# Transfers of the turned weights cut into parts and released by TensorE, in threshold attention followed by a bilinear FFN

## The chip, the cores and the metric

The kernel runs on one core of one Trainium2 chip. The metric is the device time of one execution in microseconds (us); less is better.

## The reference

```python
# 8 batches, 8 heads, 576 rows, head size 64; 4608 tokens, d_model 512, d_ff 1536; all float32
scores = scale * np.matmul(q, k.transpose(0, 1, 3, 2))
thresh = np.max(scores, axis=-1, keepdims=True) - tau
scores = np.where(scores >= thresh, scores, -1000000000.0)
scores = scores - np.max(scores, axis=-1, keepdims=True)
attn = np.exp(scores)
attn = attn / (np.sum(attn, axis=-1, keepdims=True) + 1e-09)
attn_out = np.matmul(attn, v)
x = np.ascontiguousarray(attn_out.transpose(0, 2, 1, 3)).reshape(B * S, H * D)
out = (x @ w_a) * (x @ w_b) @ w_out
```

## The kernel before, in words

Two heads of one batch make a **pair**; there are 32 pairs, four to a batch. The 576 query rows of a pair are handled as four **units** of 128 rows (u = 0 to 3) and one of 64 rows (u = 4, the tail). A list written out by hand orders the 160 units: for the first batch u = 0 and 1 of all four pairs, then u = 2 and 3 of each pair, then the four tails; for every later batch u = 0, 1 of each of its pairs, then u = 2, 3 and the tail of each. So a batch takes 20 units, and batches begin at units 20, 40, 60 and so on.

The main loop runs over **slots** g, one unit each. `keep_order` pins every engine to the order in which the program issues its instructions, so that what is written here as "later in the slot" is later in the queue of that engine. In slot g:

- `scores` (L325) multiplies q by k for unit g into two PSUM tiles `sc`, and VectorE takes the row maxima (L332).
- `turn_back` issues the load of `wT`, the turned weights of a part whose pieces have been written to the DRAM scratch `swap` (L460). `exchange_blocks` follows.
- `turn_blocks` transposes the 32x32 blocks of unit g-1 on VectorE (L429, for a tail L442) and, for u = 1 and u = 3, issues four DMAs of 288 KB `swap<-tw` (L437); for a tail it issues four of 72 KB (L449). `tw` is the tile in which the weights of two neighbouring units lie side by side. It has two buffers, so that the weights two tiles on may be written only when these DMAs have read theirs. Also the four tails of the first batch share one `tw` tile; later tails have a tile `wt` of one buffer.
- `advance(PORTIONS[0] * pace)` runs a share (0.3) of the FFN work due in this slot. The FFN is a generator whose products (`pab` L574, `po` L617 and L661) fill TensorE between the attention's own.
- `weigh` lets ScalarE compute exp (L359, L360) and VectorE mask and sum (L363), which frees the two `sc` tiles. Then `prep` transposes q and k of a coming pair, `advance` runs another share (0.35), and `weighted` multiplies the turned weights of unit g-4 by v (`pv`, L475), where that unit completes a part.
- The weights are normalised (L382). Then come the loads of q or k for a coming pair (L143, four DMAs of 72 KB), of v (L158, 288 KB) and the stores of finished rows (L685), and `advance` twice (0.15 and 0.2).

q is loaded four slots ahead of its pair's first unit and k three slots ahead; for a batch that begins at slot G these loads lie in the slots G-4 to G+3, q in the even ones and k in the odd ones. The first eight units of the first batch are turned on TensorE instead (`turn_pe`) and use no `swap`.

All of these DMAs but two small ones at the start are issued by SyncE, whose queue is called SPq in the profile. A `wT` load must wait until the `swap` writes that it reads have landed, and SPq stands still during such a wait. PSUM has four tiles (`banks`), handed out in turn to `sc`, `pab`, `pv` and `po`.

Of the kernel before, what the change touches and what calls it, by code (L numbers as in the profile page):

```python
# [51 lines left out]
def kernel(  # L52
# [38 lines left out]
    nc = tc.nc  # L91
    B, H, S, D = q.shape
    P = 128
    Q = 32
# [317 lines left out]
    def part(i, u):  # L412

        if i < HP:
            return {1: (i, 0), 3: (i, 1), NT: (i, 2)}.get(u)
        return {1: (i, 0), NT: (i, 1)}.get(u)

    def width(i, h):
        return (HALF, HALF, TAIL)[h] if i < HP else (HALF, HALF + TAIL)[h]

    def turn_blocks(i, u):

        ws, _ = weights.pop((i, u))
        if u < NT:
            if u % 2 == 0:
                tbufs[i] = state["tw"]
            tb = tbufs[i]
            for w in ws:
                nc.vector.transpose(w, w)  # L429
            if u % 2 == 0:  # L430
                return
            h = u // 2
            n = width(i, h)
            swap = scratch.tile([2 * NB, Q, n], FP32, tag=f"swap{n}", name="swap")
            swaps[i, h] = swap
            for g in range(G):
                nc.sync.dma_start(  # L437
                    swap[:, :, g * 2 * Q:(g + 1) * 2 * Q].rearrange("c p w -> p c w"),
                    tb[g * Q:(g + 1) * Q])
        else:  # L440
            tb = ws[0]
            nc.vector.transpose(tb, tb)  # L442
            if i < HP:
                swaps[i, 2] = scratch.tile([2 * NB, Q, TAIL], FP32, tag="swapt", name="swap")
            swap = swaps[part(i, u)]
            for g in range(G):
                c = slice((1 - g // 2) * NB, (2 - g // 2) * NB)
                w0 = swap.shape[2] - TAIL + (g % 2) * Q
                nc.sync.dma_start(swap[c, :, w0:w0 + Q].rearrange("c p w -> p c w"),  # L449
                                  tb[g * Q:(g + 1) * Q])  # L450
        if part(i, u):
            ready.append(part(i, u))

    def turn_back():

        while ready:
            i, h = ready.pop(0)
            n = width(i, h)
            wT = work.tile([P, NSLOT, n], FP32, tag="wT", bufs=WT_BUFS, name="wT")
            nc.sync.dma_start(wT, swaps.pop((i, h)).rearrange("(s r) p w -> (r p) s w", r=G))  # L460
            turned[i, h] = wT

    def join(out, lo, hi):
        nc.scalar.copy(out, lo)
# [44 lines left out]
    def weighted(i, h):  # L509

        b, hp = pairs[i]
        n = width(i, h)
        pv = product(turned.pop((i, h)), loaded[i]["v"], n)
        if h < 2:
            if hp == 0:
                x_of[b, h] = x_tile("xT")
            lo, hi = (pv[:, r, 0:HALF].rearrange("p (i t e) -> p i t e", t=2, e=Q) for r in range(2))
            join(x_of[b, h][:, hp, :].rearrange("p (t i e) -> p i t e", t=2, e=Q), lo, hi)
            if hp == HP - 1:
                complete.append((x_of.pop((b, h)), ("half", b, h)))  # L520
        if n % HALF:
            t = b % GT
            if hp == 0 and t == 0:
                xtail_of[b // GT] = x_tile("xt")
            join(xtail_of[b // GT][:, hp, t * TAIL:(t + 1) * TAIL], pv[:, 0, n - TAIL:n], pv[:, 1, n - TAIL:n])
            del loaded[i], prepared[i]
            if hp == HP - 1 and t == GT - 1:
                complete.append((xtail_of.pop(b // GT), ("tail", b - t, 0)))
# [166 lines left out]
    def advance(cols):  # L695
        running["owed"] += cols
        while running["owed"] > 0:
            if running["ffn"] is None:
                if not blocks:
                    running["owed"] = 0.0  # L700
                    return
                running["ffn"] = ffn(*blocks.pop(0))
                running["left"] = cost()
            step, rest, whole = next(running["ffn"], (None, 0, 0))
            if step == 0:
                running["owed"] = 0.0
                return
            if step is None:
                running["ffn"] = None
                state["through"] += 1  # L710
            else:
                running["owed"] -= step
                running["left"] -= step
                running["done"] = running["done"] + step if rest else 0
                running["rest"] = rest
                running["room"] = min(ROOM, whole // 2)

    def make_room():

        while running["rest"] and not (running["done"] >= running["room"] <= running["rest"]):  # L720
            owed = running["owed"]
            running["owed"] = 0.0
            advance(1)
            running["owed"] += owed - 1
# [35 lines left out]
    for g in range(len(units) + PV_LAG):  # L760
        written = len(pending)
        state["converted"] = state["added"]
        here = g < len(units)
        converting = bool(early.get(g)) or bool(early.get(g - 1))
        if here:
            i, u = units[g]
            scores(i, u)
        turn_back()
        exchange_blocks()
        pace = (PACE if g > BY_PE else PACE_EARLY) * BLOCK_COLS  # L770
        if g > BY_PE:
            pace = min(pace, backlog() / (min([a for a in arrivals if a > g] + [len(units) + PV_LAG + 1]) - g))
        pace += (NSLOT + 1) // 2 * S / (NT + 1) + CATCH_UP * max(backlog() - BLOCK_COLS, 0)
        if 2 <= g < BY_PE + 2:
            weighted_unit(*units[g - 2])
            running["owed"] -= (NSLOT + 1) // 2 * P
        if g < 3:
            prep_copy(*prep_pe(g + 1, "q"))
        convert_rest(g, 0)
        if g == 3:  # L780
            for c in range(0, NSUM - 2 * CW + 1, 2 * CW):
                extra.append(sums_u32[:, c:c + 2 * CW].rearrange("p (f w) -> p f w", w=2))
        load_weights(RAWS)
        if g > BY_PE and g <= len(units):
            turn_blocks(*units[g - 1])
        if g > BY_PE:
            advance(PORTIONS[0] * pace)
        if here:
            weigh(i, u)
        if here and g < BY_PE:  # L790
            reciprocal(i, u, nc.vector)
        if 0 < g <= BY_PE:
            turn_pe(*units[g - 1])
        if g < 3:
            prep_copy(*prep_pe(g + 1, "k"))
        for p in range(HP, NPR):
            for name, d in (("q", 2), ("k", 1)):
                if g == first[p] - d:
                    prep(p, name)
        if g > BY_PE:  # L800
            advance(PORTIONS[1] * pace)
            n = g - PV_LAG
            if BY_PE <= n < len(units) and part(*units[n]):
                make_room()
                weighted(*part(*units[n]))
                running["owed"] -= (NSLOT + 1) // 2 * width(*part(*units[n]))
        for n in early.get(g, [])[:1]:
            convert_first(n)
            convert_clamp(n)
        if here and g < BY_PE:  # L810
            diagonals(i, u)
        elif here:
            reciprocal(i, u, nc.scalar if converting else nc.vector)
            normalise(i, u)
        convert_rest(g, 1)
        if g <= BY_PE:
            advance(pace)
        convert_rest(g, 2)
        for n in early.get(g, [])[1:]:
            convert_first(n)  # L820
            convert_clamp(n)
        load_weights(RAWS)
        for p in range(HP, NPR):
            for name, d in (("q", 4), ("k", 3)):
                if g == first[p] - d:
                    load(p, name)
        for p in range(1, NPR):
            if g == first[p] - 1:
                load_v(p)
        store(written)  # L830
        if g > BY_PE:
            advance(PORTIONS[2] * pace)
            advance(PORTIONS[3] * pace)

        if not converting and not state["sums"]:
            state["slots"] = state.get("slots", 0) + 1
            for n in {1: (0,), 2: (1,), 3: (2,)}.get(state["slots"], ()):
                for z in range(2):
                    weight_sums(n, z)
            if state["slots"] >= 3 and state["through"]:  # L840
                for z in range(2):
                    weight_sums(3, z)
                state["sums"] = True
# [38 lines left out]
```

## Time and profile before

| | |
|---|---|
| median of 3 runs | 1473.05 us (1471.87 to 1476.86) |
| span of the profiled execution | 1471.9 us |
| TensorE busy (PE) | 1420.3 us, 97% of the span |
| VectorE (DVE), ScalarE (ACT), GpSimd (POOL) busy | 942.8, 678.4, 334.6 us |
| DMA queue of SyncE | 216.52 MB in 621968 packets, 67.6% of 16 engines' span |
| `swap<-tw` | 240 DMAs of 288 KB, median 5.2 us from issue to landing |
| `swap<-tw` and `swap<-wt` of tails | 16 and 112 DMAs of 72 KB, 4.3 and 2.5 us |
| `wT<-swap` | 28 of 1440 KB, 7.7 us; 32 of 1152 KB, 6.2 us; 4 of 288 KB, 4.0 us |

The profile lists no device time of its own for the profiled execution beside this span; the span agrees with the lowest of the three runs and is 1.2 us below their median. A DMA that is issued on SyncE shows on SPq with the time that the issue took, which includes the time for which the queues were too full to take it; when its data landed is told apart.

### The profile page before, as it was taken

To read this page: it belongs to the slowest core of one execution; us is meant where nothing else is said; L and a number is where in the kernel's file an instruction comes from. 1 tells how busy PE (TensorE), PEld (TensorE's weight loads), DVE (VectorE), ACT (ScalarE), POOL (GpSimd) and SP (SyncE) were. 2 spreads that over 40 slices of the span, in tenths; PEclk is the share of its full clock that TensorE was granted. 3 is DMA by queue.
4 is the path that set the end of the run, shared out by engine and by line. 5 is a ranking of instruction groups with operands and counts; after the bars stand their busy time and mean duration, and the time that the engine had idled before them with its cause. 6 is when DMAs were issued, how large, how long until landed. Compare 5 with 4: busy or idle time off the path is not lost.

```text
span 1471.9 us, 57132 instructions
## 1 busy us (share of the span) xinstructions
PE 1420.3 (97%) x25344; PEld 1210.9 (82%) x25344; DVE 942.8 (64%) x2097; ACT 678.4 (46%) x1243; POOL 334.6 (23%) x504
## 2 busy tenths in 40 slices
PE   5878999999999999999999999999999999999998
PEld 4777677887879898897888998889888888888886
DVE  5998677677766875776656765577656766613212
ACT  5886455555544554544434544354544544411010
POOL 2773503122030403031212212120404040410000
PEclk9999999999999999999999999999999999999999
DMA  9977898789858876895647876588757977530000
GB/s 189 223 187 187 176 179 193 169 173 185 198 143 166 184 191 142 168 192 141 147 97 147 180 172 149 118 189 185 161 126 143 197 169 162 132 90 16 2 17 16
DMA packets 624582, 220.75 MB, mean 150 GB/s; under 512 B 542928, under 2 KB 612048, under 8 KB 624336
## 3 DMA queue, kind: packets, MB, share of 16 engines
q1 hardware_dynamic: 621968, 216.52, 67.6%
q8 instruction: 199, 3.26, 0.9%
q10 hardware_dynamic: 2368, 0.59, 0.2%
q14 instruction: 47, 0.39, 0.1%
HBM read 127.40 MB, written 89.65 MB: 147 GB/s over the span
## 4 chain that ended last, share of the span: by engine, by line
PE 86%; DVE 6%; DMA 3%; issue 1%; ACT 1%; SPq 1%; DVEq 0%; ACTq 0%
PE pab L574 47%; PE po L617 19%; PE sc L325 10%; PE pv L475 9%; PE po L661 1%; DVE mx L332 1%; DVE tw L363 1%; DVE tw L429 1%; DMA swap<-tw 1%; SPq L437 1%; DMA sums_u<-in_moe_w_a_dram 1%; DVE low L238 1%; DMA kT<-in_k_dram 0%; DMA wT<-swap 0%; PE tp L402 0%
## 5 line engine op out<-in xcount | busy, mean ns | idle before, releaser
L332 DVE TENSOR_REDUCE mx<-sc 128x1 f32<-128x576 f32 x288 | 205.2, 749 | 116.5 <-PE sc L325 105.7
L574 PE MATMUL pab<-xS,wa_sb 64*64 64x256 f32 (+1 forms) x3584 | 274.4, 373 | 1.9 <-issue 1.8
L574 PE MATMUL pab<-xS,wb_sb 64*64 64x256 f32 (+1 forms) x3584 | 266.6, 369 | 0.0
L325 PE MATMUL sc<-kT,qT 64*64 64x288 f32 x2304 | 243.4, 410 | 20.7 <-DVE kT L312 9.1
L574 PE MATMUL pab<-xT,wa_sb 64*64 64x256 f32 (+1 forms) x3200 | 238.2, 370 | 7.2 <-DVE tw L363 3.2
L586 POOL TENSOR_TENSOR h<-h 128x256 f32<-128x256 f32 x168 | 117.3, 732 | 548.0 <-PE po L617 544.9
L617 PE MATMUL po<-wo_sb,h 64*64 64x256 f32 x3264 | 240.7, 376 | 0.0
L574 PE MATMUL pab<-xT,wb_sb 64*64 64x256 f32 (+1 forms) x3200 | 237.0, 369 | 3.6 <-DVE h L582 2.2
L382 ACT ACTIVATE tw<-tw,rcp 128x576 f32<-128x576 f32 x244 | 176.1, 768 | 133.8 <-DVE rcp L376 133.6
L360 ACT ACTIVATE tw<-sc,bias,scalars 128x576 f32<-128x576 f32 x260 | 216.3, 832 | 17.4 <-DMA swap<-tw 6.5
L574 PEld LDWEIGHTS pab<-xS,wa_sb 64*64 64x64 f32 x3584 | 196.6, 134 | 29.7 <-issue 3.0
L363 DVE SCALAR_TENSOR_TENSOR tw<-sc,thr,tw 128x576 f32<-128x576 f32 x260 | 203.8, 802 | 22.5 <-ACT tw L360 21.8
L574 PEld LDWEIGHTS pab<-xS,wb_sb 64*64 64x64 f32 x3584 | 194.1, 133 | 23.0 <-issue 0.2
L574 PEld LDWEIGHTS pab<-xT,wa_sb 64*64 64x64 f32 x3200 | 171.9, 133 | 31.1 <-DVE kept L465 4.3
L617 PEld LDWEIGHTS po<-wo_sb,h 64*64 64x64 f32 x3264 | 177.7, 132 | 23.6
L574 PEld LDWEIGHTS pab<-xT,wb_sb 64*64 64x64 f32 x3200 | 172.3, 133 | 25.2 <-DVE h L582 2.4
L475 PE MATMUL pv<-wT,vm 64*64 64x320 f32 (+3 forms) x2592 | 186.8, 377 | 1.7 <-DVE h L582 1.7
L325 PEld LDWEIGHTS sc<-kT,qT 64*64 64x64 f32 x2304 | 145.2, 134 | 52.4 <-issue 17.2
L617 PE MATMUL po<-sums_u,h 64*64 64x256 f32 x2448 | 180.9, 376 | 0.0
L429 DVE STREAM_TRANSPOSE tw<-tw 128x576 f32<-128x576 f32 x240 | 171.6, 753 | 0.0
L582 DVE TENSOR_TENSOR h<-h,pab 128x512 f32<-128x512 f32 (+1 forms) x112 | 73.4, 655 | 145.3 <-PE pab L574 140.3
L475 PEld LDWEIGHTS pv<-wT,vm 64*64 64x64 f32 x2592 | 143.6, 133 | 20.9 <-DVE h L582 2.6
(83 smaller groups left out, 1240.8 us busy)
## 6 DMA issues: line engine op xcount, KB each, us to landing
swap<-tw SPq DMA_DIRECT2D x240, 288.0 KB, 5.2
wT<-swap SPq DMA_DIRECT2D x28, 1440.0 KB, 7.7
wT<-swap SPq DMA_DIRECT2D x32, 1152.0 KB, 6.2
vm<-in_v_dram SPq DMA_DIRECT2D x32, 288.0 KB, 4.8
qT<-in_q_dram SPq DMA_DIRECT2D x112, 72.0 KB, 3.6
kT<-in_k_dram SPq DMA_DIRECT2D x112, 72.0 KB, 4.9
swap<-wt SPq DMA_DIRECT2D x112, 72.0 KB, 2.5
out_dram<-kept SPq DMA_DIRECT2D x30, 256.0 KB, 4.7
```

The costliest lines, as they stand in the source:

```text
L238: nc.vector.scalar_tensor_tensor(out=low, in0=hi, scalar=0x80000000, in1=low, op0=ALU.bitwise_and, op1=ALU.bitwise_or)
L325: nc.tensor.matmul(sc[j if u < NT else 0][to, c], qT[r, q0:q0 + D], kT[r, c * SH:(c + 1) * SH], start=True, stop=True)
L332: nc.vector.tensor_reduce(mx[:, c], sc[j], axis=AX.XY, op=ALU.max)
L360: nc.scalar.activation(wb[j], sb[j], AF.Exp, bias=bias[:, j:j + 1], scale=e_scale)
L363: nc.vector.scalar_tensor_tensor(out=wv, in0=sb[j], scalar=thr[:, j:j + 1], in1=wv, op0=ALU.is_ge, op1=ALU.mult, accum_out=sums[:, j:j + 1])
L382: nc.scalar.activation(w, w, AF.Copy, scale=rcp[:, j:j + 1])
L429: nc.vector.transpose(w, w)
L475: nc.tensor.matmul(pv[j * D:(j + 1) * D, r], vm[rows, k0], wT[rows, k0], start=(s == (NT if j == r else 0)), stop=(s == NT - 1))
L574: nc.tensor.matmul(pab[c * D:(c + 1) * D, r], w[rows, f // n, k, fs + c * D:fs + (c + 1) * D], moving, start=(k == 0), stop=(k == H - 1))
L582: nc.vector.tensor_tensor(ht, ht, pab, op=ALU.mult)
L586: (nc.vector if state["over"] else nc.gpsimd).tensor_tensor(*a, **kw)
L617: nc.tensor.matmul(po[c * D:(c + 1) * D, r, y], ht[rows, t0:t0 + D], other[rows, f], start=(f == 0), stop=(f == NF // 2 - 1))
```

## The change

The DMAs of the turned weights are no longer issued where they are made. They are put in a list `bulk`: each of the four 288 KB writes of a `swap` as an item of its own, the four 72 KB writes of a tail together as one item, and each `wT` load cut into three items of three slots (480, 384 or 96 KB each). A new function `pump` takes the oldest item, looks up the TensorE instruction that the program issued last, and issues the item's DMAs with a semaphore wait of the first of them on that instruction. `pump` is called at four places of a slot from slot 9 on: after `turn_blocks`; after the first `advance`; after `weighted`, ahead of the loads of q, k and v and of the stores; and between the last two `advance`. Ahead of `weighted`, what is left of the part that it needs is issued at once.

```diff
             for g in range(G):
-                nc.sync.dma_start(
-                    swap[:, :, g * 2 * Q:(g + 1) * 2 * Q].rearrange("c p w -> p c w"),
-                    tb[g * Q:(g + 1) * Q])
+                bulk.append((None, [(swap[:, :, g * 2 * Q:(g + 1) * 2 * Q].rearrange("c p w -> p c w"),
+                                     tb[g * Q:(g + 1) * Q])]))
...
+            bulk.append((None, []))
             for g in range(G):
...
-                nc.sync.dma_start(swap[c, :, w0:w0 + Q].rearrange("c p w -> p c w"),
-                                  tb[g * Q:(g + 1) * Q])
+                bulk[-1][1].append((swap[c, :, w0:w0 + Q].rearrange("c p w -> p c w"), tb[g * Q:(g + 1) * Q]))
...
-            nc.sync.dma_start(wT, swaps.pop((i, h)).rearrange("(s r) p w -> (r p) s w", r=G))
+            rows = swaps.pop((i, h)).rearrange("(s r) p w -> (r p) s w", r=G)
+            for s in range(0, NSLOT, 3):
+                bulk.append(((i, h), [(wT[:, s:s + 3], rows[:, s:s + 3])]))
             turned[i, h] = wT
+
+    bulk = []
+
+    def pump(count=1):
+
+        for _ in range(min(count, len(bulk))):
+            behind = next(x.name for x in reversed(nc.cur_bb.bb.instructions) if x.engine == mybir.EngineType.PE)
+            for n, (out_, in_) in enumerate(bulk.pop(0)[1]):
+                done = nc.sync.dma_start(out_, in_)
+                if n == 0:
+                    tc.add_manual_dep(
+                        done.ins, behind,
+                        mybir.DependencyInfo(mybir.DependencyClass.Sync, mybir.DependencyReason.DATA),
+                        reason="pace")
...
             turn_blocks(*units[g - 1])
         if g > BY_PE:
+            pump()
             advance(PORTIONS[0] * pace)
+            pump()
         if here:
             weigh(i, u)
...
                 make_room()
+                while part(*units[n]) in [whose for whose, _ in bulk]:
+                    pump()
                 weighted(*part(*units[n]))
                 running["owed"] -= (NSLOT + 1) // 2 * width(*part(*units[n]))
+            pump()
...
             advance(PORTIONS[2] * pace)
+            pump()
             advance(PORTIONS[3] * pace)
```

## The prediction

> **What bounds the kernel now.** I read the page's busy shares and its chain first, then the windows of a few stretches, then the timeline of SyncE's queue and of ScalarE.
>
> ```profile
> PE 1420.3 (97%) x25344; PEld 1210.9 (82%) x25344; DVE 942.8 (64%) x2097; ACT 678.4 (46%) x1243; POOL 334.6 (23%) x504
> PE 86%; DVE 6%; DMA 3%; issue 1%; ACT 1%; SPq 1%; DVEq 0%; ACTq 0%
> ```
>
> TensorE bounds it: 97% busy, 86% of the chain. What DMAs can give back is in the 3%. The windows tell where.
>
> ```profile
> 146.00:194.00 48.00, 46.57 (x727) 33.37 (x723) 34.04 (x79) 21.93 (x41) 18.71 (x17) 1.00 0.85 176
> 194.00:235.00 41.00, 39.10 (x688) 28.37 (x684) 29.58 (x67) 20.80 (x37) 0.00 (x0) 0.96 0.92 186
> 347.00:379.00 32.00, 29.80 (x484) 24.53 (x483) 20.73 (x47) 13.84 (x26) 1.64 (x5) 0.95 0.94 199
> 695.00:738.00 43.00, 43.00 (x791) 37.56 (x787) 27.50 (x61) 20.81 (x36) 12.26 (x21) 1.00 0.56 127
> ```
>
> The columns are the window, its length, busy time of PE, PEld, DVE, ACT, POOL, granted clock, DMA share and GB/s. Where a batch begins (slots 16 to 24, 24 to 28, 44 to 47) the DMA engines are 85 to 94% busy and TensorE loses 1.4, 1.9 and 2.2 us; in the fourth window DMA is at 56% and TensorE loses nothing. So transfers matter only near a batch's start. ScalarE shows what is late there, the exp of a unit behind the `swap` that must first have read its tile:
>
> ```profile
> 203.79 0.83 ACT L360 ACTIVATE tw<-sc,bias,scalars 128x576 f32<-128x576 f32 x1 [0.38 <-DMA swap<-tw]
> 221.60 0.83 ACT L360 ACTIVATE tw<-sc,bias,scalars 128x576 f32<-128x576 f32 x1 [2.16 <-DMA swap<-tw]
> 365.34 0.83 ACT L360 ACTIVATE tw<-sc,bias,scalars 128x576 f32<-128x576 f32 x1 [3.91 <-DMA swap<-tw]
> ```
>
> In SyncE's queue I look at what stands between a `swap` and the `wT` that reads it. First the tails of the first batch (slots 17 to 21), then the second pair of batch 2 (slots 42 to 44):
>
> ```profile
> 159.71 0.38 SPq L460 DMA_DIRECT2D wT<-swap  x1
> 160.13 5.10 SPq L449 DMA_DIRECT2D swap<-tw  x4
> 165.28 2.28 SPq L143 DMA_DIRECT2D kT<-in_k_dram  x4
> 167.94 0.38 SPq L460 DMA_DIRECT2D wT<-swap  x1
> ...
> 182.64 3.11 SPq L449 DMA_DIRECT2D swap<-tw  x4
> 185.79 3.11 SPq L143 DMA_DIRECT2D qT<-in_q_dram  x4
> 188.95 0.50 SPq L685 DMA_DIRECT2D out_dram<-osb  x1
> 189.61 1.32 SPq L460 DMA_DIRECT2D wT<-swap  x1
> ```
>
> ```profile
> 335.89 5.62 SPq L437 DMA_DIRECT2D swap<-tw  x4
> 341.61 5.58 SPq L143 DMA_DIRECT2D qT<-in_q_dram  x4
> 347.37 0.38 SPq L460 DMA_DIRECT2D wT<-swap  x1
> ```
>
> The loads of q and k fill the time in which a `swap` lands, so `wT` hardly waits; the queue goes without a pause, about a slot behind TensorE.
>
> **What the Trainium skill says.** "DMA: Bandwidth & Descriptors", Two DMAs through the same engine are not ordered: the issuing engine has to wait for the first DMA's semaphore before it issues one that reads its data. The trace agrees: L460 waited for `swap<-tw` 76.1 us in 35 times between 215 and 1320 us. The same page, Anatomy of one DMA, gives some 2 us of fixed cost per DMA, mostly completion, and says that the wait is the issuing sequencer's (measured there on GpSimd's path). Here a lone tail issued at 724.19 (2.59 us) let `wT` go at 728.49, 1.7 us after the last issue. "TensorE: Matmul & The Clock Gate", Part 1: after an idle window the array's clock is halved for a few us. The trace has it: 0.95 over 32 us and 0.96 over 41 us are 1.6 us lost each.
>
> **The change part by part.**
>
> *More instructions.* 64 `wT` loads become 192, 128 more, at 0.38 us each 49 us of SyncE, which between batch starts stands idle for part of every slot (nothing from 720.6 to 724.2, for instance). There it costs nothing; at a batch's start 0.8 us per load are in the sums below. The waits are 240 + 32 + 192 = 464, so up to as many more semaphore increments on TensorE. "TensorE: Matmul & The Clock Gate", The cost: per-tile semaphore tail, prices one at 26 ns: an upper estimate of 12.2 us if each held the array. The chain shows 757 products of `pab` in 40.80 us, 53.9 ns each, with twelve tile ends in them for which ScalarE or VectorE wait, and no break. I take 0, range 0 to 12.
>
> *Later release between batch starts.* A `swap`'s four parts took 4.4 to 4.7 us to issue anyway (715.90, 4.67) and landed 4 us later, with two slots (16 us) until the tile is needed. Spread over four places up to 0.8 of an 8 us slot, the last lands at about 12 us. Hidden; 0, and no gain since nothing waited.
>
> *Order at a batch's start.* This is the cost. The last part of a `swap`, and a whole tail of the first batch (the three parts of the `wT` before it take the first three places), move to the fourth place, behind the loads of q or k and the stores. It lands later by those loads' issue time, and the next thing in the queue is the `wT` that must wait for it: SyncE stands still for the landing, with nothing behind it able to go, where the loads used to fill that time.
>
> (a) Tails, slots 17 to 21. SyncE's step from `wT` to `wT` is now (189.61 - 159.71) / 4 = 7.5 us, and a slot of TensorE 6.6 to 7. After: `wT` 1.2, loads 2.8 (mean of 2.28, 2.16, 3.56, 3.11), tail 3.6 (5.10, 3.36, 2.73, 3.11), landing 1.7 to 2.7, taken as 2.2, store 0.3: 10.1 us, 2.6 more. Four steps are 10 us, and the first `wT` is itself 3 us late (its `swap`'s last part behind q). The last tail lands some 13 us later than now. Exp of slot 22, which must await it, starts at 189.40 after 1.29 us of idle that a DMA ended (the view names qT, which exp does not read; the tails' tile is what it needs), so it has no slack. TensorE runs on about 2 us before PSUM is full: **11 us**.
>
> (b) The next `swap` of that batch (194.04, 5.84 us, before exp at 203.79): behind q's 3.74 us, plus a bare landing. SyncE's lag is mostly the stall already counted, so I take 4 less the 1 us that TensorE runs on: **3 us**.
>
> (c) Batch 2: the last part behind 5.58 us of q, so exp of slot 44 goes at 351.7 instead of 346.2. At 365.34 a delay of 3.91 cost TensorE 1.82 + 0.38 and half clock after; 5.5 us cost about 4: **4 us**. The exp at 365.34 keeps its delay: SyncE and TensorE are both 4 us later.
>
> (d) Half clock after the stalls of (a), (b), (c), 1.6 each, less one where stalls adjoin: **4 us**.
>
> (e) Batches 3 to 7: the same 3.2 to 5.1 us of q, but the landing of that `swap` lies 2 to 7 us ahead of its exp (497.8 against 503.3, for instance), so **0**, up to 2 each.
>
> Sum 11 + 3 + 4 + 4 = 22 us on the profiled 1471.9: 1494. The median stands 1.2 above this span, so **1495 us**. The unknown ends: if landings cost 1.7 and TensorE's slack is 3 us at each stall, 13 us; if the lag of batch 1 carries on and increments cost a third of their bound, 40 us.
>
> **Rivals.** (1) *Nothing moves.* Where SyncE is a slot late, the waits on TensorE are over before it comes to them, and PSUM and the two-slot margin take up the reordering. For it: ScalarE waits for a `swap<-tw` only three times, 6.5 us in all. Against: at 203.79 the margin was 0. 1473 us, give or take 4.
>
> (2) *Faster.* Loads of 72 KB no longer stand behind four writes and a `wT` of 1440 KB, and the queue in front of a batch's third pair is shorter; the waits at 221.60 and 365.34 go. Their price is 1.52 + 0.38 and 1.82 + 0.38 us of idle TensorE, 3.2 us of half clock, and 1.40 us before the scores at 171.93: 8.7 us, 1464. It decides if the last part of the `swap` of slot 44 lands before 361.4. Against: no byte is saved, DMA is 94% busy there, and a new standstill comes ahead of it.
>
> (3) *Much slower.* A landing after q takes 3 us more than I think, margins of batches 3 to 7 fall too, each 2 to 3 us and half clock: 1495 + 5 x 4 = 1515.
>
> **How the numbers follow.** My case 0.67, (1) 0.15, (2) 0.11, (3) 0.07. My case reaches from 1486 (13 us) to 1513 (40 us). The range from 1471 to 1513 leaves out rival 2, the lower half of rival 1 and most of rival 3. About 0.3% (4.4 us) is what a measurement of this kernel can tell from no change. Faster by more 0.12, within 0.16, slower 0.72.
>
> **What would show it.** On SPq, q or k between the third and the fourth `swap` part, and `wT` (first of three) waiting 2 us or more behind a tail at 165 to 210 us, steps near 10 us. On ScalarE, L360 waiting for `swap<-tw` in slot 22 (10 us or more) and slot 44. PE windows after slot 48 full as before, `pab` still at 53.9 ns. I am wrong if step times in slots 17 to 21 stay near 7.5 us, or if TensorE is slower by a little in every window (increments), or if the waits at 221.60 and 365.34 vanish.

## The result, and the profile after

The changed kernel takes 1485.62 us (median of 4 runs, 1485.1 to 1489.0) against 1472.46 us for the kernel before in the same comparison: a ratio of 1.010, 95% interval 1.0075 to 1.0124. It is slower by 13 us by the medians and by 14.7 by the ratio (11 to 18 by its interval), where 22 were forecast. The profiled execution is the slowest of the four (1489.0 us, span 1487.2), so the two profiles differ by 15.3 us, some 2 more than the medians. 1.8 us of that lie ahead of slot 9 (the scores of slot 8 start at 75.57 and 77.42 us), where the change touches nothing.

The page of the changed kernel, busy shares and chain:

```profile
PE 1427.4 (96%) x25344; PEld 1188.3 (80%) x25344; DVE 941.6 (63%) x2097; ACT 678.0 (46%) x1243; POOL 334.7 (23%) x504
PE 87%; DVE 4%; DMA 3%; issue 2%; ACT 2%; SPq 2%; ACTq 0%; DVEq 0%
```

The same work, the same bound; TensorE's share fell from 97 to 96%. The windows that answer to those of before, moved by about the delay so that they hold nearly the same work; by their counts the second and third hold 12 and 18 products fewer (window, length, busy PE, PEld, DVE, ACT, POOL, clock, DMA share, GB/s):

```profile
148.00:208.00 60.00, 51.32 (x728) 34.90 (x724) 33.93 (x79) 22.63 (x41) 18.72 (x17) 0.92 0.70 144
208.00:247.00 39.00, 37.27 (x676) 27.13 (x672) 29.12 (x64) 19.78 (x36) 0.00 (x0) 0.99 0.86 184
361.00:393.00 32.00, 29.01 (x466) 22.17 (x462) 20.28 (x46) 14.71 (x26) 0.85 (x3) 0.95 0.83 189
709.00:752.00 43.00, 43.00 (x791) 37.72 (x787) 26.93 (x61) 20.96 (x37) 12.29 (x21) 1.00 0.57 125
```

Nearly all of it is in the first, slots 16 to 22: 8.7 us of idle TensorE instead of 1.4, and a clock of 0.92 over 60 us, 4.8 us more. That is 12.1 us. The DMA engines, 85% busy there before, are 70% busy now: they wait as well. The second window has lost nothing more, the third 0.8 us more of idle, the fourth nothing.

How late TensorE is can be read without windows, from VectorE's first row maxima of a slot (L332), which follow its scores:

| slot | before, us | changed, us | later by |
|---|---|---|---|
| 21 | 179.65 | 181.02 | 1.4 |
| 23 | 194.90 | 208.93 | 14.0 |
| 28 | 234.90 | 247.10 | 12.2 |
| 44 | 344.40 | 356.87 | 12.5 |
| 46 | 359.78 | 377.14 | 17.4 |
| 48 | 379.07 | 393.08 | 14.0 |
| 159 | 1280.96 | 1296.33 | 15.4 |

So 12.7 us are lost by slot 23 and 1.8 of them won back by slot 28. Batch 2 costs 5 us at first and 1.5 in the end, because the kernel before has a wait of its own there. The rest of the run adds 1.4.

SyncE's queue in slots 16 to 21, and in slots 42 to 44:

```profile
160.26 0.44 SPq L471 DMA_DIRECT2D swap<-tw  x1
163.81 1.45 SPq L471 DMA_DIRECT2D wT<-swap  x3
165.30 3.81 SPq L143 DMA_DIRECT2D kT<-in_k_dram  x4
169.15 3.52 SPq L471 DMA_DIRECT2D swap<-tw  x4
174.27 1.44 SPq L471 DMA_DIRECT2D wT<-swap  x3
...
195.20 2.10 SPq L143 DMA_DIRECT2D qT<-in_q_dram  x4
197.35 1.14 SPq L700 DMA_DIRECT2D out_dram<-osb  x1
198.59 2.12 SPq L471 DMA_DIRECT2D swap<-tw  x4
202.44 1.44 SPq L471 DMA_DIRECT2D wT<-swap  x3
```

```profile
350.30 3.54 SPq L471 DMA_DIRECT2D swap<-tw  x3
353.90 4.97 SPq L143 DMA_DIRECT2D qT<-in_q_dram  x4
358.96 0.44 SPq L471 DMA_DIRECT2D swap<-tw  x1
362.45 1.45 SPq L471 DMA_DIRECT2D wT<-swap  x3
```

What matters is the empty time ahead of each `wT`. After the tail of 169.15 the queue stands from 172.67 to 174.27, 1.6 us; after that of 198.59, 1.7 us (after the two between, 1.8 and 1.9); after the lone last part of 160.26 it stands 3.1 us and after that of 358.96, 3.1 us. In each of these six places the last write lands 0.02 to 0.13 us before the `wT` is issued. The step from `wT` to `wT` is (202.44 - 163.81) / 4 = 9.7 us, where it was 7.5.

ScalarE, the exp of slot 22 and that of slot 44:

```profile
202.65 0.83 ACT L360 ACTIVATE tw<-sc,bias,scalars 128x576 f32<-128x576 f32 x1 [6.90 <-DMA swap<-tw]
362.54 0.83 ACT L360 ACTIVATE tw<-sc,bias,scalars 128x576 f32<-128x576 f32 x1 [3.93 <-issue]
```

ScalarE waits 6.9 us in slot 22 until the last tail has left its tile, and starts 13.3 us after the 189.40 of before. In slot 44 the profile names no releaser; the last part of the `swap` lands at 362.39. TensorE's idle times there:

```profile
186.89 0.86 PE L490 MATMUL pv<-wT,vm 64*64 64x64 f32 x33 [2.03 <-DMA wT<-swap]
191.90 2.24 PE L325 MATMUL sc<-kT,qT 64*64 64x288 f32 x13 [1.30 <-issue]
204.44 0.74 PE L490 MATMUL pv<-wT,vm 64*64 64x64 f32 x34 [4.31 <-issue]
```

The first is a `pv` whose turned weights land too late. The longest ends at 204.44; the profile names no releaser, but VectorE's masking, which frees the scores' first PSUM tile behind that late exp, ends at 204.33, while the turned weights of that `pv`, issued at 193.46, had landed by 197.2. So I read the chain as late tail, late exp, full PSUM, idle TensorE; that PSUM was full is inferred from this order of times.

### The profile page after: what moved, and what is told of

The parts are those of the page before. It is cut to its first block, busy times and chain, and to the rows that moved or that the text cites. A ratio compares the mean times of both kernels' runs of the same rounds, so it can differ in the third digit from the quotient of the medians.

```text
span 1487.2 us, 57433 instructions
## 1 busy us (share of the span) xinstructions
PE 1427.4 (96%) x25344; PEld 1188.3 (80%) x25344; DVE 941.6 (63%) x2097; ACT 678.0 (46%) x1243; POOL 334.7 (23%) x504
## 4 chain that ended last, share of the span: by engine, by line
PE 87%; DVE 4%; DMA 3%; issue 2%; ACT 2%; SPq 2%; ACTq 0%; DVEq 0%
PE pab L589 47%; PE po L632 19%; PE sc L325 10%; PE pv L490 9%; DMA swap<-tw 1%; PE po L676 1%; DVE tw L363 1%; DVE mx L332 1%; DVE tw L429 1%; DMA sums_u<-in_moe_w_a_dram 1%; ACT tw L360 1%; SPq L151 1%; DVE low L238 1%; SPq L471 0%; DMA sums_u<-in_k_dram 0%
## 5 line engine op out<-in xcount | busy, mean ns | idle before, releaser
L332 DVE TENSOR_REDUCE mx<-sc 128x1 f32<-128x576 f32 x288 | 205.0, 748 | 114.3 <-PE sc L325 103.6
L325 PE MATMUL sc<-kT,qT 64*64 64x288 f32 x2304 | 250.8, 416 | 22.5 <-DVE kT L312 8.2
L589 PE MATMUL pab<-xS,wb_sb 64*64 64x256 f32 (+1 forms) x3584 | 271.2, 370 | 0.1
L589 PEld LDWEIGHTS pab<-xS,wa_sb 64*64 64x64 f32 x3584 | 192.4, 134 | 32.9 <-issue 2.3
L490 PE MATMUL pv<-wT,vm 64*64 64x320 f32 (+3 forms) x2592 | 189.8, 379 | 8.4 <-issue 4.6
L589 PEld LDWEIGHTS pab<-xT,wb_sb 64*64 64x64 f32 x3200 | 169.2, 133 | 29.2 <-DVE h L597 2.9
```

Source lines behind the costliest of these rows:

```text
L325: nc.tensor.matmul(sc[j if u < NT else 0][to, c], qT[r, q0:q0 + D], kT[r, c * SH:(c + 1) * SH], start=True, stop=True)
L332: nc.vector.tensor_reduce(mx[:, c], sc[j], axis=AX.XY, op=ALU.max)
L490: nc.tensor.matmul(pv[j * D:(j + 1) * D, r], vm[rows, k0], wT[rows, k0], start=(s == (NT if j == r else 0)), stop=(s == NT - 1))
L589: nc.tensor.matmul(pab[c * D:(c + 1) * D, r], w[rows, f // n, k, fs + c * D:fs + (c + 1) * D], moving, start=(k == 0), stop=(k == H - 1))
```

## The experiments

My theory after this: the loss is the **order** of SyncE's queue. A tail or a last part stands behind the loads and its `wT` right behind it, so that the queue stands still for each landing. The rivals: the waits on TensorE, or the cuts of `wT`.

**The changed kernel without its waits.**

```diff
-                if n == 0:
+                if False:
                     tc.add_manual_dep(
```

> The changed kernel without the waits on TensorE: the same parts in the same order on SyncE. If the order is the cause (a tail and the last part of a swap behind the loads, the wT right behind them), nothing comes back: 1483 to 1488 us, and SyncE still steps some 9.5 us from wT to wT in slots 17 to 21. If the waits on TensorE hold the transfers back, it returns to 1473 give or take 3, with steps of 7.5 us.

Measured: 1487.83 us, ratio to before 1.0101 (1.0086 to 1.0116), as slow as with them. Window and step of its trace:

```profile
148.00:208.00 60.00, 50.27 (x722) 34.85 (x718) 33.65 (x77) 22.15 (x40) 18.69 (x17) 0.93 0.69 142
```

```profile
162.63 1.45 SPq L471 DMA_DIRECT2D wT<-swap  x3
...
202.69 1.44 SPq L471 DMA_DIRECT2D wT<-swap  x3
```

The `wT` of slots 17 and 21 start at 162.63 and 202.69, steps of 10.0 us. The waits do no harm that these runs can tell. In the changed kernel they hold SyncE for some 249 us in 224 waits (125.8, 55.0, 52.4 and 15.4 us on `pab`, `po`, `sc` and `pv`); as the time stays the same without them, SyncE had that time to spare.

**The fourth place ahead of the loads.**

```diff
-            pump()
+            pump(2)
...
             advance(PORTIONS[2] * pace)
-            pump()
```

> The changed kernel with its fourth place moved ahead of the loads of q, k and v (two items at the third place, none at the fourth): all cuts and all waits on TensorE stay. If the order is the cause, 1472 to 1477 us, since the loads again fill the landing. If the waits or the cuts are the cause, it stays at 1483 to 1488.

Measured: 1473.50 us, ratio 1.0008 (0.9998 to 1.0018). All waits and cuts are still there, and the loss is gone. SyncE's queue for the same tails:

```profile
167.42 2.19 SPq L471 DMA_DIRECT2D wT<-swap  x3
169.66 2.14 SPq L471 DMA_DIRECT2D swap<-tw  x4
171.84 2.16 SPq L143 DMA_DIRECT2D qT<-in_q_dram  x4
174.04 0.50 SPq L700 DMA_DIRECT2D out_dram<-osb  x1
174.70 1.49 SPq L471 DMA_DIRECT2D wT<-swap  x3
```

The loads again lie between a tail and its `wT`, and 0.2 us is left of the pause. SyncE's waits for `swap<-tw` tell the same story over the whole run, in the order before, changed, without waits, fourth place ahead:

```profile
SPq L460 <- DMA swap<-tw: 84.8, 41, 4.8
```

```profile
SPq L471 <- DMA swap<-tw: 130.1, 46, 5.2
```

```profile
SPq L471 <- DMA swap<-tw: 132.3, 47, 5.2
```

```profile
SPq L471 <- DMA swap<-tw: 89.6, 38, 5.1
```

The columns are us in total, times and the longest. There are 45 us more with the new order, with or without the waits on TensorE. The sum alone prices nothing, though: it is 117.1 us with the early loads below, which make the kernel faster. It matters where the queue stands.

**One move at a time, in the kernel before.** The first batch's tails go to the slot's end; or the fourth part of each `swap`; or both; or `wT` is only cut.

The cut shows the tails; for the fourth part the condition is `g == G - 1`.

```diff
...
+                if i < HP:
+                    late.append(put)
+                else:
+                    nc.sync.dma_start(*put)
...
             advance(PORTIONS[2] * pace)
+            while late:
+                nc.sync.dma_start(*late.pop(0))
```

> The kernel before with one thing moved: the four tails of the first batch are issued at the slot's end, behind the loads; no cuts, no waits on TensorE. If the tails' order makes most of the loss, 1481 to 1486 us (8 to 13 more than before), TensorE late by slot 23. If it takes the cuts or waits as well, 1473 give or take 3.

> The kernel before with the fourth 288 KB part of every swap issued at the slot's end, behind the loads; no cuts, no waits on TensorE, tails as before. By the prediction's terms (b), (c) and their half clock 1480 to 1484; by the trace of the changed kernel, where these places took only 1 to 2 us, 1474 to 1477. If the order does nothing here, 1473 give or take 2.

> The kernel before with both moves at once: the first batch's tails and the fourth part of every swap at the slot's end, behind the loads; no cuts, no waits on TensorE. If the two moves together are the whole cause, 1484 to 1488 us, more than their separate losses of 6.2 and 4.8 us, because the fourth part of the swap of slot 16 delays the start of the tails' row. If the losses only add up, 1482 to 1485. If the cuts of wT are needed as well, clearly less than 1482.

> The kernel before with each wT load issued as three DMAs in its old place. If 0.38 us per issue is the only price, it is covered: 1472 to 1475 us. If the cuts carry part of the loss, 1476 or more.

| kernel | median us | ratio to before | us by the ratio |
|---|---|---|---|
| tails late | 1479.18 | 1.0037 (1.0022 to 1.0052) | 5.4 |
| fourth parts late | 1477.77 | 1.0030 (1.0015 to 1.0045) | 4.4 |
| both late | 1482.12 | 1.0073 (1.0047 to 1.0098) | 10.7 |
| `wT` cut only | 1474.01 | 1.0013 (1.0002 to 1.0023) | 1.9 |

Both moves make 10.7 us. They add up within their intervals; that they would do more together than apart isn't shown. The fourth parts alone came out between the two ranges that I had given. The tails alone cost less than the 8 to 13 us that I had expected: their row then starts at 158.67, as before, and not 5 us late. In their trace TensorE does come 9 us later from slot 16 to slot 23 (against before), but 4.5 of them are gone by slot 48, behind the two places at which the kernel before waits itself. The cuts are not quite free: each `wT` takes 1.45 us of SyncE's queue and not 0.38. Their 1.9 us (0.3 to 3.4) bring the sum to 12.6, against the 14.7 of the change by the same kind of ratio; the intervals overlap, and are too wide to say that nothing else costs. Where in the run the cuts cost it, the profile doesn't show.

**Later landing, or standstill?** The tails stay late, but their `wT` goes behind the loads too.

Part `h == 2` exists in the first batch alone and holds a pair's tail; its `wT` is put in the list ahead of the next tail.

```diff
...
+            if h == 2:
+                late.append(put)
+            else:
+                nc.sync.dma_start(*put)
```

> The kernel of the late tails (four tails of the first batch behind the loads), with the wT loads of those tails put behind the loads as well, so that a slot's loads lie between a tail and the wT that reads it. If the standstill of SyncE for the landing is the cost, its step returns to about 7 us and the time to 1470 to 1474 us. If the later landing of the tails itself is the cost, it stays with the late tails, 5 to 7 us over before.

Measured: 1472.09 us, ratio 0.9995 (0.9986 to 1.0005).

```profile
165.48 2.28 SPq L842 DMA_DIRECT2D swap<-tw  x4
167.87 2.76 SPq L143 DMA_DIRECT2D qT<-in_q_dram  x4
170.73 0.44 SPq L693 DMA_DIRECT2D out_dram<-osb  x1
171.35 0.38 SPq L842 DMA_DIRECT2D wT<-swap  x1
171.78 2.53 SPq L842 DMA_DIRECT2D swap<-tw  x4
```

The tails are as late in their slot as with the late tails alone, only the load right behind them is another. From the second `wT` (171.35) to the fifth (193.36) the step is 7.3 us; with the late tails alone it is 9.5 ((196.62 - 158.67) / 4), with 3.2 us of standstill in its first:

```profile
164.30 2.37 SPq L838 DMA_DIRECT2D swap<-tw  x4
169.86 0.38 SPq L464 DMA_DIRECT2D wT<-swap  x1
```

The exp of slot 22, first with the late tails alone and then with `wT` behind the loads:

```profile
196.66 0.83 ACT L361 ACTIVATE tw<-sc,bias,scalars 128x576 f32<-128x576 f32 x1 [8.02 <-DMA swap<-tw]
192.78 0.83 ACT L361 ACTIVATE tw<-sc,bias,scalars 128x576 f32<-128x576 f32 x1 [5.00 <-DMA kT<-in_k_dram]
```

The loss over the run is gone. In place it is not quite: the later tails still make that exp wait 5.00 us, where it waited 1.29 before, and TensorE comes some 3.5 us later by slot 23. That is won back by slot 28, behind the wait that the kernel before has at 221.60. So it is the standstill that makes most of the loss and all that stays of it, not the place of the tail by itself.

**Relieving a batch's start.** Does the reading lead to a faster kernel? q and k of later batches are loaded in the idle stretch; or every `wT` goes behind its slot's loads; or both; or the early loads go with the fourth place ahead.

```diff
-                if g == first[p] - d:
+                if g == first[p] - d - (5 - p % HP if p >= 2 * HP else 0):
                     load(p, name)
```

```diff
-            nc.sync.dma_start(wT, swaps.pop((i, h)).rearrange("(s r) p w -> (r p) s w", r=G))
+            late.append((wT, swaps.pop((i, h)).rearrange("(s r) p w -> (r p) s w", r=G)))
...
             advance(PORTIONS[2] * pace)
+            while late:
+                nc.sync.dma_start(*late.pop(0))
```

> The kernel before, with q and k of the batches from the third on loaded up to five slots sooner, where DMA is little used (q of a batch's four pairs in slots G-9, -6, -3 and 0 instead of G-4, -2, 0 and 2, k one slot later each). If ScalarE waits at a batch's start because loads stand ahead of a swap in a full queue, the wait at 365 us goes with its half clock: 1467 to 1470 us. If the transfers of the swaps alone fill the queue there, 1473 give or take 2.

> The changed kernel with the fourth place ahead of the loads, and with the early loads of q and k for the batches from the third on. If both reliefs are real and add up, 1465 to 1469 us. If they remove the same stall, no better than the early loads alone.

> The kernel before with every wT load issued at its slot's end, behind the loads. If SyncE's waits for landings cost anything in the kernel before, 1467 to 1470 us; if the loads cover them already, 1471 to 1474; if wT comes too late for its product two slots on, slower than that.

> The early loads of q and k together with every wT load at its slot's end. If both help, 1464 to 1468 us; if the early loads leave no wait for the other to save, as the early loads alone, about 1469.

| kernel | median us | ratio to before |
|---|---|---|
| early loads | 1469.49 | 0.9988 (0.9979 to 0.9997) |
| early loads, fourth place ahead | 1470.25 | 0.9991 (0.9983 to 0.9999) |
| every `wT` behind the loads | 1468.74 | 0.9972 (0.9952 to 0.9991) |
| both `wT` behind and early loads | 1467.13 | 0.9958 (0.9943 to 0.9973) |

With every `wT` behind the loads alone 4.1 us come back (1.3 to 7.1), so SyncE's waits for landings cost something in the kernel before too. The last is faster than both kernels: 6 us under before. In its trace TensorE gains 1.6 us by slot 28 and 4.8 more by slot 48, at the starts of batches 1 and 2. SyncE at the start of batch 2 in its trace:

```profile
330.90 4.75 SPq L438 DMA_DIRECT2D swap<-tw  x4
335.75 2.52 SPq L158 DMA_DIRECT2D vm<-in_v_dram  x1
340.20 0.38 SPq L835 DMA_DIRECT2D wT<-swap  x1
345.95 4.41 SPq L438 DMA_DIRECT2D swap<-tw  x4
```

The queue has gaps between its transfers where it had none before, and ScalarE's waits for `swap<-tw`, 6.5 us before, are absent from this trace's list. The early loads alone came out in the range expected, and the wait at 365 us and its half clock are gone from their trace; but the kernel before was at 1471.21 us in that comparison, so that they gave 1.8 us and not 3 to 6. That the relief adds to the fourth place ahead isn't shown.

## Why the prediction was right or wrong

The stated range held. But 1485.6 us lies just below the 1486 at which my own case began: the mechanism was right and its price too high.

*Order at a batch's start, the mechanism.* Right, in the form in which it was written: loads between the third and the fourth part, `wT` right behind, the queue standing still for the landing. The kernels with the fourth place ahead, with the waits taken out and with `wT` behind the loads show it from three sides.

*(a) Tails.* The step was forecast at 10.1 us and is 9.7; exp of slot 22 was to be 13 us late and is 13.3. The term was 11 us of idle TensorE, and the window shows 7.3 more. The rest of the 12.1 us lost there is half clock, which has its own term. I had one wait in mind; there are three, the first a `pv` that waits for `wT`.

*(d) Half clock.* 4 us in all. The first window has 4.8 more, the second 1.2 less (0.99 for 0.96), the third the same: 3.6. The sum was right, its place was not; that these errors cancel is luck.

*(b) The next `swap` of that batch.* 3 us were forecast, and the window after slot 23 shows none (1.7 us idle, 1.9 before); TensorE even wins 1.8 us back by slot 28. The exp in question does wait, 1.60 us at 219.06 for 0.38 at 203.79, but TensorE was 14 us late by then: the stall of (a) had paid for it. I named this and still took 3.

*(c) Batch 2.* 4 us were forecast, and TensorE ends 1.5 us later than it came in (slots 44 and 48), with 0.8 more of idle in the window, which opens 1.5 us too late. Exp of slot 44 does wait, 3.93 us at 362.54. But the step "the exp at 365.34 keeps its delay" failed: its wait fell from 3.91 to 2.16 us, as this line of the changed kernel shows.

```profile
381.04 0.83 ACT L360 ACTIVATE tw<-sc,bias,scalars 128x576 f32<-128x576 f32 x1 [2.16 <-PE pab L589]
```

A stall taken earlier gives the queue time, and the next one shrinks by it. (b) and (c) are the same error, and they make 5 to 6 of the 9 us by which the forecast is too high (by the medians); (a) makes most of the rest.

*(e) Batches 3 to 7 and the release between them.* 0 forecast, up to 2 each, and the fourth window is full as before. It was not quite 0: at the start of batch 7 two exps wait, 1.98 us at 1184.79 and 2.50 at 1201.42, where one waits 1.16 before, and TensorE is 0.9 us later after them. *Semaphore increments:* 0 taken, 12 as the bound; the kernel with all of them and the fourth place ahead stands at 1.0008, and the changed kernel's chain again has 757 products of `pab` in 40.80 us. *More issues:* 0 taken, 1.9 measured.

*Rivals.* That nothing moves would have been right for the waits on TensorE alone, whose cost can't be measured here. The faster rival fell: the two waits that it wanted gone are still there. That of 365.34 is the 2.16 us above, and that of 221.60 is this one, 2.00 us for 2.16:

```profile
235.49 0.83 ACT L360 ACTIVATE tw<-sc,bias,scalars 128x576 f32<-128x576 f32 x1 [2.00 <-PE pab L589]
```

Those of 6.90 and 3.93 us have come on top.

## What to carry to other kernels

On a queue that is issued in order, look at what stands between a transfer and the one that must wait for it. Unrelated loads there use the time of the landing; a move that takes them out makes the queue, and all that is behind it, stand still for each landing. The waits on TensorE cost nothing that could be measured here; the order did. When several stalls follow one another in the same queue, the first pays for part of the next, so their prices are not to be summed.

## What was not expected of the hardware

The standstill behind a lone 288 KB write (3.1 us, at 160.26 and 358.96) is longer than the 1.6 to 1.9 us behind four of 72 KB in the same trace. The four loads of q ahead of it are part of that: they were issued earlier but landed only by 161.82 and 360.67, and the write landed 1.9 and 1.7 us after them, at 163.69 and 362.39. So what the queue stands for includes the transfers still on their way. How much of it the write's own size makes isn't shown.

About 7 us more of idle TensorE in a few pieces (2.03, 1.30 and 4.31 us the longest) brought a further 4.8 us lost to half clock, two thirds of the idle time again. The pieces need not be long: the granted clock is 0.50 from 188.3 to 195.1 us, behind an idle time of 2.03 us that ended at 186.89. In the kernel before it is 0.50 from 368.6 to 372.0 us, behind pieces of 1.82 and 0.38 us.
